# Attention steps 3 to 6 each followed by two half tiles of the first layer, and the row statistics of tile 2 made once

## The chip, the core and the metric

The program runs on one core of a Trainium2 chip. The core has five engines that work side by side and wait for each other through semaphores: TensorE (PE) multiplies matrices and writes to PSUM, VectorE (DVE) and ScalarE (ACT) do elementwise work, GpSimd (POOL) does a little of it, and SyncE (SP) issues most transfers between HBM and SBUF. The metric is the device time of one execution in microseconds (us); lower is better.

## What is computed

Three stages, each on the result of the one before, all in fp32:

```python
# 1 attention with a decaying state: B=4, H=8, S=768, D=64
for t in range(S):
    state = gamma * state + einsum('bhd,bhe->bhde', k[:, :, t], v[:, :, t])
    y[:, :, t] = scale * einsum('bhd,bhde->bhe', q[:, :, t], state)
x = y.transpose(0, 2, 1, 3).reshape(3072, 512)
# 2 first feed-forward block, d_ff = 1024
h = x @ w_in
sm = exp(h - h.max(-1)) / (sum(exp(h - h.max(-1)), -1) + 1e-9)
solu = h * sm
ln = (solu - mean(solu)) / sqrt(var(solu) + 1e-6) * g_ln
x = ln @ w_out
# 3 second feed-forward block, d_ff = 2048
h = x @ w_in2
out = (h * cos(h)) @ w_out2
```

## The kernel before

The attention is cut into 24 **steps** of 64 positions for two batches and all heads (`step`, called by `attend`). A step multiplies its queries with the state, its masked scores with the values, adds its keys and values to the state (`S`) and, in its second half, makes the scores (`sc`) of the next step. On PE it is 64 rows of the order, 128 matmuls of 64x64 in the trace (lines L409, L415, L427). Its result `y` is split by ACT into a high part `xh` and by DVE into a low part `xl`; the two are tile n of the first layer, 128 tokens. Tiles 2 and 3 keep them in `o1h` and `o1l`.

The **first layer** (`mm1`, L633) takes a tile in two halves, c = 0 and c = 1, of 512 columns each: 12 matmuls of 128x512 into one PSUM bank (`xh` times `w1h`, `xl` times `w1h`, `xh` times `w1l`, for four k). Tiles 0, 2 and 4 write to the three banks of `hB`, the others to the two of `hA`. Tile 0 has banks 0 and 1 of `hB`, tile 2 banks 1 and 2, so that the c = 0 half of tile 2 takes the bank of tile 0's c = 1 half. `norm` (L643) makes the row statistics of a whole tile: a maximum on DVE (`sm`, L651), an exponential on ACT (`u`), a product on DVE (`u<-u,hB`, L362), a square on ACT (`junk`), a power on POOL, a normalisation on ACT or DVE (L664), with small one-column operations between. Its product is the last that reads the bank. `first(n, c)` does one half and calls `norm` when c is 1; `chunk` does a quarter of a half and calls `norm` when c is 0 and the last k is done.

The normalised tiles are transposed on PE (`transp`, L678, into `tr`, whose banks take the place of `hB`), split by ACT and DVE into `lt`, and multiplied by the second layer's weights (`mm2`, L703, into `y1`). Beside this ACT and DVE convert weights out of 64-bit words (`convert`, `split_w`): first those of this block (`big`), then those of the second block (`raw`, `wt`, stages `st`), which go back to HBM and are read there from some 320 us on. The second block (L879, L960) fills the rest of the time.

What sets the order: nothing is issued as it is written. Every operation goes into a `Plan`, which holds PE's order to the written one but for a window of 10, and picks on the other engines what can start first and has the longest tail. It works with costs in its own tables; `FETCH` tells it how long PE waits for the next block of 256 instructions, with its first number a time at which the cost changes. The instructions are then built engine by engine in the order found, and each engine runs its own in that order. So a call that is moved in the text moves PE's work directly and reorders the other engines.

Of the kernel before, what the change touches and what calls it, by code (L numbers as in the profile page):

```python
# [32 lines left out]
KD = DM // 128  # L33
# [15 lines left out]
class Plan:  # L49
# [17 lines left out]
    LOOK = .1  # L67
    FIRST = (16, 0.97, 0.6)
    BLOCK = (63, 256)
    FETCH = (30.0, 6.3, 4.0)  # L70

    def __init__(self):
        self.ops = []
# [49 lines left out]
    def order(self):  # L123
# [62 lines left out]
        while left:  # L186
# [36 lines left out]
            if e == "PE":  # L223
# [3 lines left out]
                if fetched[0] // self.BLOCK[1] > was:  # L227
                    blocks.append(max(t + occ, blocks[-1]) + self.FETCH[1 if t < self.FETCH[0] else 2])
            else:
# [28 lines left out]
def body(ctx: ExitStack, tc: tile.TileContext, qkv, consts,  # L258
# [126 lines left out]
    def prep(n):  # L385
        i = steps[n][1]
        if i:
            P.add("POOL", 1.2, lambda: nc.gpsimd.tensor_tensor(  # L388
                out=a_p[n % 2].rearrange("p (a b) t -> p a b t", b=2),
                in0=a_q[n % NA].rearrange("p (a b) t -> p a b t", b=2),  # L390
                in1=gat.unsqueeze(2).to_broadcast([128, NHP, 2, C]), op=ALU.mult),
                [("gat",), ("in", n % NA, 1)], [("x32", n % 2)], port=True)
        if has_state(n):
            k = a_kn[n % NA]
            for a in range(NHP):
                f = cs[:, 1, i, a:a + 1]
                act(k[:, a], k[:, a], AF.Copy, [("cs",), ("in", n % NA, 2)], [("ks", n % NA, a)], 0.295,
                    alt=("DVE", 0.2, lambda k=k[:, a], f=f: nc.vector.tensor_scalar(
                        out=k, in0=k, scalar1=f, scalar2=None, op0=ALU.mult), True), scale=f)
# [225 lines left out]
    def mm1(n, c, k, ms=(0, 1, 2)):  # L625
        h, hk = hbank(n, c)
        xh, xl = xhs[xb(n)], xls[xb(n)]
        xhk, xlk = xk[xb(n)]

        def mm():  # L630
            for m in ms:
                a, lo = ((xh, 0), (xl, 0), (xh, 1))[m]
                nc.tensor.matmul(out=h, lhsT=a[:, k], rhs=w1[lo][k][c], start=(k + m == 0), stop=(k == KD - 1 and m == 2))  # L633
        r = [xhk]
        if 0 in ms or 1 in ms:
            r += [("w1h", k, c)]
        if 1 in ms:
            r += [xlk]
        if 2 in ms:
            r += [("w1l", k, c)]  # L640
        P.add("PE", 0.2267 * len(ms), mm, r, [hk], lat=0.2267 * len(ms) + 0.25, ni=2 * len(ms))
# [374 lines left out]
    def load_to(n):  # L1016
        while loaded[0] <= min(n, ns - 1):
            load_step(loaded[0])
            loaded[0] += 1
# [6 lines left out]
    def weights(n):  # L1026
        for _ in range(min(n, len(wq))):
            f, args = wq.pop(0)
            f(*args)
# [3 lines left out]
    def attend(ahead=True):  # L1033
        n = nxt[0]
        if n >= ns:
            return
        nxt[0] += 1
        if n > 3:
            load_to(n + 1)
        if n + 1 < ns and ahead:  # L1040
            prep(n + 1)
        step(n, ahead)
        if n == ns - 1:
            p2["sb_hook"] = [P.add("HOOK", 0.0, open_sb, lat=0.0, after=P.using({"in", "ag", "asc", "ast", "sc", "S", "y", "wt", "stg", "top"}))]

    def first(n, c):
        for k in range(KD):
            mm1(n, c, k)
        if c == 1:
            norm(n)  # L1050

    def chunk(c, k, tiles=(0, 1)):
        for ms in ((0, 1), (2,)):
            for n in tiles:
                mm1(n, c, k, ms)
                if c == 0 and k == KD - 1 and 2 in ms:
                    norm(n)
# [18 lines left out]
    attend()  # L1076
    for k in range(KD):
        chunk(1, k, (1,))
    attend(False)
    P.chained(True)  # L1080
    load_to(4)
    P.chained(False)
    for k in range(KD):
        chunk(0, k, (0,))
    first(2, 1)
    prep(3)
    scores(3)
    for k in range(KD):
# [3 lines left out]
    attend()  # L1092
    first(2, 0)
    norm(2)
    attend()
    first(3, 0)
    attend()
    first(3, 1)
    weights(len(wq))
    first(4, 0)  # L1100
    first(4, 1)
    attend()
    first(5, 0)
    transp(0, 0)
    transp(0, 1)
    first(5, 1)
    attend()
    transp(0, 2)
    transp(0, 3)
    mm2(0, 0, None, range(2))  # L1110
# [149 lines left out]
```

## Time and profile before

| | |
|---|---|
| median of 3 runs | 839.0 us (837.82 to 840.07) |
| profiled execution | 837.1 us, span 835.3 us |
| PE busy | 817.4 us, 98% of the span |
| DVE, ACT, POOL busy | 649.0, 506.4, 48.6 us |
| transfers | 188.19 MB, mean 225 GB/s |

The span goes from the first to the last instruction; the profiled execution's own time is 1.8 us longer. Attention and first block fill it to about 318 us, the second block from there on. Busy time of PE is modelled and counts matmuls that overlap, so its share is no measure of how tight its work stands: that is read from the starts of its matmuls, and from the time in brackets that a row of the timeline shows when the engine was idle before it.

### The profile page before, as it was taken

The page shows a single profiled execution, that of the slowest core. Times are in us where ns is not written, and L with a number is a line of the kernel's source. Part 1 is how long each engine was busy: PE and PEld are TensorE (multiplying, and loading weights), DVE is VectorE, ACT ScalarE, POOL GpSimd, SP SyncE. Part 2 cuts the span into 40 slices and gives each one's busy share as a digit, 9 for nine tenths or more (in the row PEclk, how much of TensorE's full clock was granted, in tenths as well). Part 3 has the DMA queues.
Part 4 walks back from the last instruction along what each step waited for, and adds up shares of the span by engine and source line. Part 5 has one row for each costly group of instructions (what it writes and reads, how often), then busy time and mean ns, then how long its engine had stood idle before and what let it go on. Part 6 is the DMA issues. An engine that isn't in the chain of part 4 may idle for free.

```text
span 835.3 us, 18919 instructions
## 1 busy us (share of the span) xinstructions
PE 817.4 (98%) x7312; PEld 717.0 (86%) x7312; DVE 649.0 (78%) x1157; ACT 506.4 (61%) x893; POOL 48.6 (6%) x56
## 2 busy tenths in 40 slices
PE   5899999999999999999999999999999999999997
PEld 4778888888888888888889999888999988889997
DVE  4789988879888677338789993787999648779953
ACT  4688857656666466346785463676746446665452
POOL 2221210111101000000000000000000000000000
PEclk9999999999999999999999999999999999999999
DMA  9893699899976649246665688767667787666563
GB/s 353 326 336 114 194 320 342 270 322 300 323 271 224 219 161 319 86 131 195 192 207 184 198 257 246 233 192 197 201 195 209 198 271 194 196 191 188 181 193 83
DMA packets 93513, 188.19 MB, mean 225 GB/s; under 512 B 9712, under 2 KB 25328, under 8 KB 93424
## 3 DMA queue, kind: packets, MB, share of 16 engines
q1 hardware_dynamic: 92816, 186.41, 70.1%
q8 instruction: 58, 0.95, 0.5%
q10 hardware_dynamic: 608, 0.57, 0.2%
q14 instruction: 31, 0.25, 0.1%
HBM read 145.01 MB, written 41.94 MB: 224 GB/s over the span
## 4 chain that ended last, share of the span: by engine, by line
PE 90%; DMA 4%; DVE 3%; SPq 1%; ACT 1%; issue 1%; ACTq 0%
PE U L879 27%; PE pa L960 15%; PE hA L633 13%; PE y L703 11%; PE U L960 8%; PE pb L960 4%; PE y L427 4%; PE hB L633 2%; PE tr L678 2%; PE tr L703 2%; DMA big<-w_in_dram 1%; DMA in<-qkv_dram 1%; PE sc L409 1%; DVE u L362 1%; DMA y1d<-ys 1%
## 5 line engine op out<-in xcount | busy, mean ns | idle before, releaser
L960 PE MATMUL pa<-wr,gh 128*128 128x256 f32 x768 | 139.8, 283 | 0.0
L902 ACT ACTIVATE gh<-A 128x512 fp32r<-128x512 f32 x144 | 90.7, 630 | 78.6 <-PE pa L960 43.6
L904 DVE TENSOR_TENSOR gl<-A,gh 128x512 fp32r<-128x512 f32 x144 | 98.6, 686 | 29.7 <-ACT gh L902 29.6
L960 PEld LDWEIGHTS pa<-wr,gh 128*128 128x128 f32 x768 | 120.2, 192 | 0.5
L960 PE MATMUL pa<-wr,gl 128*128 128x256 f32 x384 | 108.7, 283 | 0.0
L703 PE MATMUL y<-lt,o1h 128*128 128x512 f32 x304 | 101.9, 399 | 0.0
L960 PEld LDWEIGHTS pa<-wr,gl 128*128 128x128 f32 x384 | 73.7, 192 | 0.0
L960 PE MATMUL U<-wr,gh 128*128 128x256 f32 x384 | 70.3, 283 | 0.0
L703 PEld LDWEIGHTS y<-lt,o1h 128*128 128x128 f32 x304 | 57.1, 188 | 12.2
L633 PE MATMUL hA<-w1h,xh 128*128 128x512 f32 x160 | 64.4, 403 | 0.3 <-DVE u L362 0.2
L633 PE MATMUL hA<-w1l,xh 128*128 128x512 f32 x160 | 62.5, 391 | 0.0
L633 PE MATMUL hA<-w1h,xl 128*128 128x512 f32 x160 | 62.4, 390 | 0.0
L960 PEld LDWEIGHTS U<-wr,gh 128*128 128x128 f32 x384 | 59.9, 192 | 0.0
L703 PE MATMUL y<-lt,o1l 128*128 128x512 f32 x152 | 59.3, 390 | 0.0
L351 ACT ACTIVATE st<-wt 128x512 fp32r<-128x512 f32 (+1 forms) x60 | 35.8, 601 | 33.7 <-DMA wd<-st 17.8
L960 PE MATMUL U<-wr,gl 128*128 128x256 f32 x192 | 54.3, 283 | 0.0
L354 DVE TENSOR_TENSOR st<-wt,st 128x512 fp32r<-128x512 f32 (+1 forms) x60 | 40.5, 678 | 17.0 <-ACT st L351 16.8
L427 PE MATMUL y<-s,in 64*64 64x64 f32 x736 | 45.0, 226 | 1.1 <-DVE s L354 1.1
L427 PEld LDWEIGHTS y<-s,in 64*64 64x64 f32 x736 | 36.4, 138 | 9.2 <-issue 4.6
L427 PE MATMUL y<-x,st 64*64 64x64 f32 x672 | 40.3, 218 | 0.0
L388 POOL TENSOR_TENSOR x<-in,c_all 128x512 f32<-128x512 f32 x22 | 30.5, 1385 | 141.2 <-issue 88.2
L960 PEld LDWEIGHTS U<-wr,gl 128*128 128x128 f32 x192 | 36.9, 192 | 0.0
(180 smaller groups left out, 2082.6 us busy)
## 6 DMA issues: line engine op xcount, KB each, us to landing
wr<-wd SPq DMA_DIRECT2D x168, 256.0 KB, 3.0
wr<-td SPq DMA_DIRECT2D x168, 256.0 KB, 3.0
in<-qkv_dram SPq DMA_DIRECT2D x48, 512.0 KB, 6.2
wd<-st SPq DMA_DIRECT2D x28, 512.0 KB, 4.9
td<-st SPq DMA_DIRECT2D x24, 512.0 KB, 3.5
raw<-w_in_dram SPq DMA_DIRECT2D x16, 511.8 KB, 6.0
raw<-w_out_dram SPq DMA_DIRECT2D x16, 511.8 KB, 5.0
y1d<-ys SPq DMA_DIRECT2D x24, 256.0 KB, 3.7
```

What stands on the lines that cost most here:

```text
L351: return P.add("ACT", occ, lambda: nc.scalar.activation(out=out, in_=in_, func=func, **kw), r, w, lat, alt=alt)
L354: return P.add("DVE", occ, lambda: nc.vector.tensor_tensor(out=out, in0=a, in1=b, op=op), r, w, port=port)
L362: return P.add("DVE", occ, lambda: nc.vector.scalar_tensor_tensor(out=out, in0=a, scalar=s, in1=b, op0=op0, op1=op1, **kw), r, w, port=port)
L388: P.add("POOL", 1.2, lambda: nc.gpsimd.tensor_tensor(out=a_p[n % 2].rearrange("p (a b) t -> p a b t", b=2), in0=a_q[n % NA].rearrange("p ( ...
L427: nc.tensor.matmul(out=ybank(n)[0][o, j], lhsT=a[r, j], rhs=b[r, j], start=not part, stop=bool(part) or not later)
L633: nc.tensor.matmul(out=h, lhsT=a[:, k], rhs=w1[lo][k][c], start=(k + m == 0), stop=(k == KD - 1 and m == 2))
L678: nc.tensor.transpose(out=trs[s][:, t * 128:(t + 1) * 128], in_=us[(4 * g + t) % UBUF].rearrange("p c f -> p (c f)")[:, j * 128:(j + 1) * ...
L703: nc.tensor.matmul(out=y1(), lhsT=w[:, j, ds], rhs=lts[j][:, a], start=(j + m == 0), stop=(j == K1 - 1 and m == 2))
L879: nc.tensor.matmul(out=U(), lhsT=p2["wr"][w][:, kk, lo], rhs=p2["x"][m][xl][:, kk], start=(kk + q == 0 and m in (0, 1, 4)), stop=(kk == 1 ...
L902: P.add("ACT", 0.54, lambda: nc.scalar.activation(out=p2["gh"][i], in_=src(), func=AF.Copy), [key], [("gh", i)], after=(*p2["cos_hook"], * ...
L904: P.add("DVE", 0.6, lambda: nc.vector.tensor_tensor(out=p2["gl"][i], in0=src(), in1=p2["gh"][i].bitcast(F32), op=ALU.subtract), [key, ("gh ...
L960: nc.tensor.matmul(out=o, lhsT=p2[x][g][:, t * 128:t * 128 + 128], rhs=v[:, lo], start=(fresh and t % 2 == 0 and i == 0), stop=(s == 7 and ...
```

## The change

In the text of the program's order, four things:

- `attend(False)`, step 2, moves from behind tile 1's c = 1 half to behind the first half of tile 0's c = 0 half.
- `first(2, 1)`, the c = 1 half of tile 2 with a `norm` behind it, becomes four calls of `chunk` with c = 1, which call no `norm`. The other `norm(2)`, behind the c = 0 half, stays.
- Steps 4 to 6 come later: an `attend()` behind tile 2 goes, the next ones stand behind the c = 0 half of tiles 3, 4 and 5, and the one behind tile 5 goes. So 7 steps in place of 8 are done ahead of the loop, and from tile 6 on each step stands one tile closer to its own tile.
- The planner's `FETCH` goes from (30.0, 6.3, 4.0) to (60.0, 5.8, 4.5).

```diff
-    FETCH = (30.0, 6.3, 4.0)
+    FETCH = (60.0, 5.8, 4.5)
...
     for k in range(KD):
         chunk(1, k, (1,))
-    attend(False)
     P.chained(True)
     load_to(4)
     P.chained(False)
-    for k in range(KD):
+    for k in range(2):
         chunk(0, k, (0,))
-    first(2, 1)
+    attend(False)
+    for k in range(2, KD):
+        chunk(0, k, (0,))
+    for k in range(KD):
+        chunk(1, k, (2,))
     prep(3)
...
     first(2, 0)
     norm(2)
-    attend()
     first(3, 0)
     attend()
     first(3, 1)
     weights(len(wq))
     first(4, 0)
+    attend()
     first(4, 1)
+    first(5, 0)
     attend()
-    first(5, 0)
     transp(0, 0)
     transp(0, 1)
     first(5, 1)
-    attend()
```

PE near 22 us, at the end of step 1 (its result goes to `hA_135`). Before, step 2 (`in2`, into `y_173`) follows at once:

```order
L427 MATMUL hA_135<-x32_1_112,st1_169 64x64 x2
L409 MATMUL sc_171<-in2_164 64x64 x2
L427 MATMUL y_173<-s0_166,in2_164 64x64 x2
L415 MATMUL S_172<-in2_164 64x64 x2
L427 MATMUL y_173<-x32_0_111,st0_168 64x64 x2
```

After, tile 1 (`xh1`, `xl1`) follows:

```order
L427 MATMUL hA_135<-x32_1_112,st1_169 64x64 x2
L409 MATMUL sc_171<-in2_164 64x64 x2
L633 MATMUL hA_135<-w1h01_86,xh1_127 128x512
L633 MATMUL hA_135<-w1h01_86,xl1_129 128x512
L633 MATMUL hA_135<-w1l01_94,xh1_127 128x512
```

Tile 1's 12 matmuls went from the middle of step 2 to its front, right behind the step that makes `xh1` and `xl1`.

DVE at the row statistics of tile 0 (`sm0`, `u0`) and of tile 2 (`sm2`, `u2`). Before:

```order
L651 TENSOR_REDUCE sm0_77<-hB_139 128x1
L651 TENSOR_REDUCE sm2_79<-hB_139 128x1
L354 TENSOR_TENSOR s1_167<-sc_171,c_all_170 128x256
L362 SCALAR_TENSOR_TENSOR u0_104,sm0_77<-u0_104,hB_139 128x1024
L362 SCALAR_TENSOR_TENSOR u2_106,sm2_79<-u2_106,hB_139 128x1024
L651 TENSOR_REDUCE sm1_78<-hA_135 128x1
```

After:

```order
L354 TENSOR_TENSOR o1l_125<-y_173,o1h_124 128x512
L651 TENSOR_REDUCE sm0_77<-hB_139 128x1
L354 TENSOR_TENSOR s1_167<-sc_171,c_all_170 128x256 x2
L398 TENSOR_SCALAR in1_163<-in1_163,c_all_170 128x128 x2
L362 SCALAR_TENSOR_TENSOR u0_104,sm0_77<-u0_104,hB_139 128x1024
```

The maximum and the product of the incomplete tile 2 are gone from between tile 0's and tile 1's.

PE behind the c = 0 half of tile 2 (`hB_139`, `o1h_124`). Before, step 4 (`in0`) follows:

```order
L633 MATMUL hB_139<-w1h30_91,o1h_124 128x512
L633 MATMUL hB_139<-w1h30_91,o1l_125 128x512
L633 MATMUL hB_139<-w1l30_99,o1h_124 128x512
L427 MATMUL y_173<-s0_166,in0_162 64x64 x2
L415 MATMUL S_172<-in0_162 64x64 x2
```

After, the c = 0 half of tile 3 (`hA_135`), and step 4 behind its 12 matmuls:

```order
L633 MATMUL hB_139<-w1h30_91,o1h_124 128x512
L633 MATMUL hB_139<-w1h30_91,o1l_125 128x512
L633 MATMUL hB_139<-w1l30_99,o1h_124 128x512
L633 MATMUL hA_135<-w1h00_85,o1h_124 128x512
L633 MATMUL hA_135<-w1h00_85,o1l_125 128x512
```

So steps 4, 5 and 6 each stand 12 matmuls later against the tiles, and two half tiles lie between one and the next.

## Rows read from the trace of the kernel before

**Rows 1.** The page: span, busy time by engine, granted clock in 40 slices.

```profile
span 835.3 us, 18919 instructions
PE 817.4 (98%) x7312; PEld 717.0 (86%) x7312; DVE 649.0 (78%) x1157; ACT 506.4 (61%) x893; POOL 48.6 (6%) x56
PEclk9999999999999999999999999999999999999999
```

**Rows 2.** PE's timeline: start us, length us, instruction, [idle before <- releaser].

```profile
22.52 0.27 PE L427 MATMUL y<-s,in 64*64 64x64 f32 x2 [0.57 <-DVE s L354]
...
41.56 0.50 PE L633 MATMUL hB<-w1h,o1h 128*128 128x512 f32 x1 [1.66 <-DVE u L362]
...
132.65 0.33 PE L678 MATMUL tr<-ident,u 128*128 128x128 f32 x1 [0.30 <-DVE lt L690]
...
308.98 0.50 PE L633 MATMUL hA<-w1h,xh 128*128 128x512 f32 x1 [0.22 <-DVE u L362]
```

**Rows 3.** The chain of waits, 34 to 42 us: start us, length us, what.

```profile
34.36 2.36 DVE sm L651 x2
...
36.81 2.31 ACT u L351 x4
...
39.14 2.38 DVE u L362 x4
```

**Rows 4.** Instructions on `u`, 30 to 50 us: count, duration ns min/median/max, starts.

```profile
L351 ACT ACTIVATE junk<-u,sm x3: 1138/1150/1150, 45.7 to 49.1; 128x1024 bf16<-128x1024 f32 x3
L351 ACT ACTIVATE u<-hB,sm x2: 1105/1111/1117, 36.8 to 37.9; 128x1024 f32<-128x1024 f32 x2
...
L664 DVE TENSOR_SCALAR u<-u,sm x1: 814/814/814, 49.8 to 49.8; 128x1024 f32<-128x1024 f32 x1
```

**Rows 5.** Timelines of ACT, DVE and PE behind step 1.

```profile
21.98 0.60 ACT L351 ACTIVATE xh<-hA 128x512 fp32r<-128x512 f32 x1 [2.26 <-PE sc L409]
...
22.91 0.68 DVE L354 TENSOR_TENSOR xl<-hA,xh 128x512 fp32r<-128x512 f32 x1
...
23.64 0.50 PE L633 MATMUL hA<-w1h,xh 128*128 128x512 f32 x1
```

**Rows 6.** PE's timeline at the gap without a releaser.

```profile
53.23 0.40 PE L633 MATMUL hA<-w1h,o1l 128*128 128x512 f32 x1
53.46 0.39 PE L633 MATMUL hA<-w1l,o1h 128*128 128x512 f32 x1
55.64 0.39 PE L633 MATMUL hA<-w1h,o1h 128*128 128x512 f32 x1 [1.79 <-issue]
```

**Rows 7.** Instruction queue q8 (packets, MB, share): span; windows 46:47, 53:54, 59:61.

```profile
q8 instruction: 58, 0.95, 0.5%
...
q8 instruction: 1, 0.02, 6.0%
...
q8 instruction: 1, 0.02, 5.8%
...
q8 instruction: 1, 0.02, 2.9%
```

**Rows 8.** Timelines of DVE and PE at the first transposes.

```profile
66.33 1.21 DVE L362 SCALAR_TENSOR_TENSOR u<-u,hB 128x1024 f32<-128x1024 f32 x1
...
67.69 1.06 PE L678 MATMUL tr<-ident,u 128*128 128x128 f32 x8
```

**Rows 9.** Busy us by window, with granted clock, DMA share and GB/s last.

```profile
30.00:62.00 32.00, 28.55 (x510) 22.95 (x510) 24.95 (x59) 22.82 (x49) 7.38 (x7) 1.00 0.85 305
62.00:80.00 18.00, 17.78 (x324) 14.64 (x322) 18.00 (x29) 15.39 (x30) 3.69 (x4) 1.00 0.43 145
```

**Rows 10.** Timelines of DVE and PE behind step 13.

```profile
153.00 0.69 DVE L354 TENSOR_TENSOR xl<-y,xh 128x512 fp32r<-128x512 f32 x1
...
153.93 0.39 PE L633 MATMUL hA<-w1h,xl 128*128 128x512 f32 x1
```

**Rows 11.** DVE's timeline: a wait for a load of `in`.

```profile
129.89 0.48 DVE L398 TENSOR_SCALAR in<-in,c_all 128x128 f32<-128x128 f32 x2 [2.36 <-DMA in<-qkv_dram]
```

More of the change, by code (lines that the diff above doesn't have):

```diff
@@ L1082, in body @@
     P.chained(False)
+    for k in range(2):
+        chunk(0, k, (0,))
+    attend(False)
+    for k in range(2, KD):
+        chunk(0, k, (0,))
     for k in range(KD):
-        chunk(0, k, (0,))
-    first(2, 1)
+        chunk(1, k, (2,))
     prep(3)
```

## The prediction, made before the change was run

> **What bounds the kernel now.** I read the profile's page first [rows 1]. The program ran 835.3 us, TensorE (PE) was busy for 817.4 of them and its granted clock reads nine tenths or more in every slice, so it ran at the upper of its two levels, 2.4 GHz. Matmuls overlap in the trace, so busy time alone could hide waits; I therefore took PE's timeline and compared the starts of neighbouring matmuls. A 128x512 matmul starts 0.23 us after the one before it (53.23 and 53.46 in [rows 6]), a whole attention step takes 2.1 us, and from 27 us to the last matmuls there are only four places where PE starts late: 1.66 us at 41.56, 1.79 us at 55.64, 0.30 us at 132.65 and 0.22 us at 308.98 [rows 2]. The change keeps every matmul, so it can only win back waits: these four are 3.97 us, and all that it brings must come from them, less what new waits it makes. Ahead of 22 us nothing on PE moves; after 310 us the work is the same and follows the first part.
>
> The wait at 41.56 is explained by the chain of waits [rows 3]. From 34.36 on, with the first issued half of tile 2 through, VectorE (DVE) makes two row maxima (2.36), ScalarE (ACT) two exponentials (2.31) and DVE two products (2.38), one after the other, and only then may PE overwrite `hB` with the second half of tile 2. One of each pair belongs to tile 0; the other is `norm(2)` called out of `first(2, 1)`, on a tile of which half is missing.
>
> The wait at 55.64 has no releaser ("issue"), so nothing that the program waits for ended there. What the trace shows is instruction traffic: queue q8 moved 58 packets of together 0.95 MB, 16 KB each [rows 7]. PE has 7312 matmuls and as many weight loads [rows 1]; 14,624 instructions over 58 packets are 252 each, and with PE's own wait instructions about 256. An attention step is 128 matmuls in the trace, that is 256 instructions or one packet, and it is used up in 2.1 us. One such packet passed in the window 46 to 47 us and one in 53 to 54, and PE went on 1.6 to 2.6 us after the second began. Counting back from the gap, 6 matmuls (12 instructions) and all but the first 12 instructions of step 5 make one packet, so that block was entered at about 50.3 and the next one could be run at 55.64: **fetching took 5.3 us there**.
>
> The Trainium skill ("Runtime: NRT & Kernel Launch", section Instruction fetch mechanics) says that the sequencer fetches the next 16 KiB page while it runs the current one and that crossing costs "one DMA tail-bump, mostly hidden". The block size agrees with the 16 KB here, "mostly hidden" doesn't at 55.64. By that rule the new order would meet no such gap; that is a rival below.
>
> **The change part by part.** I go along PE, with starts of before as the clock.
>
> 1. *Tile 1's half ahead of step 2.* Before, PE put half of step 2 at 22.52, after 0.57 us of wait, and tile 1's 12 matmuls at 23.64 [rows 2, 5]. Now the 12 come first, and their second matmul reads `xl`, which DVE writes from 22.91 on (0.60 until the next one starts at 23.51); `xh` is there at 22.58. PE is free at 21.95, can do one matmul at about 22.6 and the next at 23.6: 0.65 + 0.70 of wait in place of 0.57, so **about 0.75 lost**. It can't be a gain, since `xl` follows the same rows on DVE; at most 1.0 lost.
>
> 2. *The duplicate goes, tile 0 ends earlier.* Removed on DVE: a maximum and a product of 1.2 each (half of what the chain shows for two), the normalisation 0.8, and some eight one-column operations of some 0.07, together 3.7 us at most; on ACT an exponential and a square, 1.1 each [rows 3, 4]. More important: tile 0's last half is now issued 1.5 to 2 us ahead of the first half of tile 2, so its maximum can start near 31.7, its product ends near 35.2, and `hB` is free 5 us before PE wants it (near 40.4). **1.66 gained**, and no next wait takes its place at that point: the exponent and product of tile 1, needed for tile 3's half in `hA` that now follows at once, end by my count near 42.5, PE comes at 43.3. This margin of 0.8 us is what covers it; without it up to 0.8 comes back.
>
> 3. *Instruction blocks at steps 4 and 5.* Twelve matmuls (24 instructions) now stand ahead of step 4, and half a tile ahead of step 5. Counted on from the boundary before, one block begins 18 instructions into step 4 and ends 9 matmuls behind it: 1.95 + 2.1 = 4.1 us of PE work. The next holds 15 matmuls and most of step 5: 3.4 + 1.85 = 5.2. A fetch of 5.3 makes 1.2 + 0.1 = **1.3 of waits in place of 1.79**, a gain of 0.5. The bounds: the block entered near 45.0 found its packet in the window 46 to 47, so it was there by 49.6 at the latest (4.6) and could be after 2.6; the one entered at 55.64 has its packet in the window 59 to 61, so up to 8 us. At 2.6 both waits vanish, at 8 they are 6.7, at 6.5 (the middle of that window) 3.7. I take 5.3, the only one measured at a gap and between the ends.
>
> 4. *First transposes.* They need the normalised tiles 0 to 3 and the last product on `hB` (tile 4). Before, they stood at 67.69, 0.27 behind the pitch, because that product ran 66.33 to 67.47 [rows 8]. From 62 to 80 us DVE was busy 18.00 of 18.00 us [rows 9], so PE can't run far ahead of it. The duplicate's time on DVE fell into a time when DVE was partly idle; by counting DVE's new order, tile 4's product ends near 65.1, when PE has done 12 instead of 15 matmuls of tile 5. PE would be there at 64.7: 0.4 in place of 0.27, **0.1 lost**. If PE comes later, through part 3, this wait shrinks, so the two cover each other.
>
> 5. *Each step one tile later.* Before, step n+1 stood between step n and the first layer of tile n; now tile n follows step n directly, with 12 or 24 second-layer matmuls (2.7 or 5.4 us) and partly 8 transposes (0.87) between. So `xh`, `xl` of a step are needed at once. The trace shows the chain behind such a step, step 13 [rows 10]: DVE writes `xl` from 153.00 on, some 0.60 net, and the second matmul of the next tile starts at 153.93. The margin is 0.3 us, and in the new order a 0.60 us weight split stands in that row at step 12. Steps 12, 16 and 20 have only the 12 matmuls: I take 0.1 each, **0.3 lost**.
>
> 6. *Later waits.* The 0.30 at 132.65 came from DVE waiting 2.36 us on a load of `in` [rows 11]; the order there is another now, and the 0.22 at 308.98 is covered by the last step, which moves from 290 us to that place. **0.5 gained.** Against it, step 10 now begins where a block begins and nearly fills it: 2.1 to 3.0 us of work against a fetch of 2.6 to 5.3. A full step inside one block cost before only when the boundaries fell on both sides; I take **0.4 lost** (0 to 3.2).
>
> Sum: 1.66 + 0.5 + 0.5 gained, 0.75 + 0.1 + 0.3 + 0.4 lost: 1.1 us. The profiled execution took 837.1 us for a span of 835.3; the median of the three runs is 839.0 (837.82 to 840.07), so the profile is 1.9 below the median. 837.1 becomes 836.0, and on the median's level 839.0 becomes **837.9 us**.
>
> The weight conversion, the queue of loads on SP and the second phase I cost at nothing: the conversion's loads now start some 6 us earlier, for they no longer stand behind an `in` load that waits for step 5, and nothing on PE reads the converted weights ahead of 336 us.
>
> **Rivals.** *A, the fetches hide.* For it: all blocks between 56 and 310 us show no gap; against it: the 1.79. Then 1.3 and 0.4 stay away, the wait at the transposes grows by 0.2, and with 2.6 us gained it is 836.4. (This is what the rule on that page of the Trainium skill gives.) *B, the fetches run long*: 6.5 us each, as loads pile up there (the DMA share is 0.85 between 30 and 62 us [rows 9]): 3.7 instead of 1.3, of which part 4 covers 0.4, and it is 839.9; at 8 us each 842.9. *C, slower: just-in-time `xl`.* DVE waited 2.36 us for a load of `in` at 129.89 [rows 11], one of three such waits over 1.5 us between 110 and 170, and PE hardly noticed, since a step's result had a whole tile of time. With 0.3 of margin such a wait ahead of `xl` goes through. Seven tiles have the short cover (11, 12, 15, 16, 19, 20, 23); at 0.8 us each 5.6 are lost, 843.2. It decides from 0.5 us each on. *D, the change does less than it says*: the planner orders by its own costs and a wait of about the old size stands elsewhere before 85 us, so that nothing moves: 839.0.
>
> **How the numbers follow.** Forecast 0.42; A 0.19; B 0.17; C 0.08; D 0.14. About 0.3% (2.5 us) is what a measurement of this kernel can tell from no change. The forecast, D and most of B lie within it; A lies on the edge, and about all of A with a tail of the forecast makes faster 0.19; slower is C and the long end of B, 0.10; within 0.3% the rest, 0.71. The range goes from 835.9 (A without the 0.3 and 0.2 of parts 5 and 4) to 840.8 (a little beyond B); it leaves out C, B's long end and a thin end below.
>
> **What would show it.** Right: the chain of waits has one maximum and one exponential ahead of tile 2's second half and no gap there; the matmul `hA<-w1h,xh` near 22.6 with its neighbour a microsecond later; a gap without releaser of 0.5 to 2 us between 46 and 57; first transposes between 65 and 66.5; gaps of a few tenths in front of tiles 12, 16 and 20 ended by `xl`; the whole rest of PE's timeline shifted by about a microsecond. Wrong: gaps without releaser that sum to over 3 us or to nothing before 60 us, a gap at tile 3's first half (part 2's margin), or gaps of half a microsecond and more ended by `xl` or by a load of `in` after 85 us.

## The result, and the profile after

The changed kernel takes 846.29 us in the median (845.95 to 850.07), the kernel before beside it 838.62 us: a ratio of 1.010, with an interval of 1.007 to 1.013. It is slower by 7.7 us, where the prediction had 837.9 us and a range up to 840.8. The profiled execution took 846.28 us for a span of 844.5, 9.2 more than before. The page of the changed kernel begins (span, busy time by engine, granted clock):

```profile
span 844.5 us, 18911 instructions
...
PE 820.5 (97%) x7312; PEld 717.8 (85%) x7312; DVE 649.8 (77%) x1160; ACT 497.9 (59%) x877; POOL 51.9 (6%) x55
...
PEclk9999999999999999999999999999999999999999
```

Against [rows 1] hardly anything shows: the same 7312 matmuls, and every slice reads 9. One has to go to PE's waits. The list of what PE waited for in the changed kernel (total us, times, longest us):

```profile
PE sc L409 <- DMA in<-qkv_dram: 5.7, 1, 5.7
PE y L427 <- issue: 3.1, 1, 3.1
PE tr L678 <- DVE lt L690: 1.8, 2, 1.0
PE hA L633 <- DVE xl L354: 1.7, 1, 1.7
PE hB L633 <- ACT w1h L351: 1.7, 1, 1.7
PE hB L633 <- DVE u L362: 1.4, 1, 1.4
PE hB L633 <- ACT u L351: 1.3, 1, 1.3
PE tr L678 <- ACT ys L708: 1.2, 1, 1.2
...
PE hB L633 <- DVE sm L651: 0.3, 1, 0.3
```

Without its first row (the first load) the list sums to 13.4 us; the same list of before sums to 7.5. So 5.9 of the 9.2 us are waits that the view names. In PE's timeline (start, length, instruction, idle before it and what ended it) the first five stand here, in place of the first rows of [rows 2]:

```profile
22.50 0.50 PE L633 MATMUL hA<-w1h,xh 128*128 128x512 f32 x1 [1.70 <-DVE xl L354]
...
32.24 0.47 PE L633 MATMUL hB<-w1h,o1h 128*128 128x512 f32 x1 [0.33 <-DVE sm L651]
34.93 0.50 PE L633 MATMUL hB<-w1l,o1h 128*128 128x512 f32 x1 [1.29 <-ACT u L351]
37.99 0.50 PE L633 MATMUL hB<-w1l,o1h 128*128 128x512 f32 x1 [1.40 <-DVE u L362]
...
61.53 0.27 PE L427 MATMUL y<-s,in 64*64 64x64 f32 x2 [3.06 <-issue]
```

The wait at 41.56 is gone, as foreseen, but three waits of together 3.0 us stand between 32 and 38, inside the 12 matmuls of tile 2's c = 1 half. ACT and DVE show the other side of them: the maximum, the exponential and the product of tile 0.

```profile
30.87 1.23 DVE L651 TENSOR_REDUCE sm<-hB 128x1 f32<-128x1024 f32 x1 [0.26 <-PE hB L633]
...
33.67 1.11 ACT L351 ACTIVATE u<-hB,sm 128x1024 f32<-128x1024 f32 x1 [2.63 <-PE hB L633]
...
36.70 1.22 DVE L362 SCALAR_TENSOR_TENSOR u<-u,hB 128x1024 f32<-128x1024 f32 x1 [3.56 <-PE hB L633]
```

The maximum is done at 32.1, yet the exponential, which needs nothing else of tile 0, starts at 33.67 and waited for PE, and PE then waited for it. They take turns: PE, ACT, PE, DVE, PE. But tile 0 reads banks 0 and 1 of `hB`, and the matmuls write bank 2.

The gap at 61.53 is the successor of the one in [rows 6], with a cost behind it that the slices of the page hide. Windows on PE in the changed kernel (busy us and count of PE, PEld, DVE, ACT, POOL, then granted clock, DMA share, GB/s):

```profile
58.47:61.53 3.06, 0.00 (x0) 0.00 (x0) 1.43 (x3) 2.33 (x5) 0.00 (x0) 1.00 0.85 340
61.53:63.20 1.67, 1.67 (x21) 1.38 (x21) 1.13 (x2) 1.19 (x2) 1.09 (x1) 0.99 0.28 91
63.20:66.60 3.40, 3.40 (x10) 2.67 (x9) 3.03 (x7) 1.97 (x4) 1.13 (x2) 0.51 0.83 294
66.60:70.00 3.40, 3.40 (x63) 2.64 (x64) 3.40 (x5) 3.16 (x8) 0.00 (x0) 1.00 0.01 2
```

From 63.2 to 66.6 the granted clock was at its lower level, 1.2 GHz: from 63.19 to 66.59 the matmuls start 0.41 to 0.43 apart in place of 0.23, eight times in a row. That is 8 times 0.2, or 1.6 us more. The Trainium skill ("TensorE: Matmul & The Clock Gate", section Part 1: The HAM clock gate) says that the half rate is the default and that activity lifts it; the two levels here, 0.51 and 1.00, agree.

So of 9.2 us, 5.9 are named waits and 1.6 the lower clock; 1.7 lie in many small delays that the list doesn't name.

### The profile page after: what moved, and what is told of

It is laid out like the page before. It is cut to its first block, busy times and chain, and to the rows that moved or that the text cites. A ratio compares the mean times of both kernels' runs of the same rounds, so it can differ in the third digit from the quotient of the medians.

```text
span 844.5 us, 18911 instructions
## 1 busy us (share of the span) xinstructions
PE 820.5 (97%) x7312; PEld 717.8 (85%) x7312; DVE 649.8 (77%) x1160; ACT 497.9 (59%) x877; POOL 51.9 (6%) x55
## 4 chain that ended last, share of the span: by engine, by line
PE 67%; DMA 2%; DVE 1%; ACT 0%; SPq 0%; issue 0%; ACTq 0%
PE U L879 27%; PE pa L960 16%; PE U L960 8%; PE y L703 4%; PE pb L960 4%; PE hA L633 4%; PE tr L703 2%; DMA raw<-y1d 2%; PE tr L678 1%; PE y L427 1%; DMA out_dram<-oo 0%; DVE u L664 0%; DVE lt L690 0%; DVE raw L354 0%; SPq L823 0%; DVE oo L935 0%
## 5 line engine op out<-in xcount | busy, mean ns | idle before, releaser
L690 DVE TENSOR_TENSOR lt<-tr,lt 128x512 fp32r<-128x512 f32 x48 | 31.2, 684 | 9.6 <-ACT lt L688 9.4
```

Source lines behind the costliest of these rows:

```text
L690: P.add("DVE", 0.6, lambda: nc.vector.tensor_tensor(out=lts[j][:, 1], in0=trs[s], in1=lts[j][:, 0].bitcast(F32), op=ALU.subtract), [("hb", ...
```

## Experiments

All ratios are to the kernel before, run beside it, with their intervals; where a kernel ran once (tile cut, two more loads, the second look, store ahead) there is no interval, and its time stands beside 840.55 us, one run of the kernel before. "Changed kernel" is the kernel of this case. So that places can be compared, the table gives by how much PE falls behind the kernel before in each stretch of the profiled execution: the work that it has left at a time (its matmuls still to come, at their usual distances), less what the kernel before had left at that time. The three columns add up to the difference of the spans and are good to about half a microsecond; a minus means that PE is ahead. The profiled execution of the kernel before took 837.1 us, 1.5 less than its median beside the changed kernel, so all sums stand that much high. What stands ahead of 26 us also differs between executions of one program (-0.5 and 0.8 in the changed kernel).

| | ahead of 26 us | 26 to 68 us | behind 68 us | span |
|---|---|---|---|---|
| step 2 alone (b_step2) | 1.7 | 7.0 | 1.4 | 10.1 |
| duplicate out alone (b_dup) | 0.0 | 1.3 | 1.0 | 2.3 |
| steps 4 to 6 alone (b_steps) | -0.3 | -0.1 | 2.0 | 1.6 |
| FETCH alone (b_fetch) | -0.4 | 2.0 | 0.7 | 2.3 |
| duplicate and steps 4 to 6 (b_dupsteps) | 1.2 | 0.4 | 4.6 | 6.2 |
| the same and FETCH (a_back2) | -0.6 | 1.5 | 9.4 | 10.3 |
| changed kernel | -0.5 | 4.6 | 5.0 | 9.2 |
| again (after_2) | 0.8 | 2.3 | 7.0 | 10.1 |
| with the old FETCH (a_fetch) | 0.9 | 1.4 | 6.3 | 8.5 |
| statistics late (e_norm) | 1.2 | 1.3 | 12.6 | 15.1 |
| tile cut (e_split) | 2.0 | -1.1 | 5.9 | 6.8 |
| duplicate out, statistics late (b_order) | 0.0 | 2.9 | 4.0 | 6.9 |
| loads held (e_hold) | 0.6 | 0.3 | 6.4 | 7.3 |
| two more loads (b_more) | -0.2 | 0.6 | 0.9 | 1.2 |
| store ahead (a_ring) | -0.3 | 1.4 | 4.4 | 5.5 |
| statistics late, loads held (e_both) | 0.3 | -1.1 | 11.6 | 10.8 |
| the same, old FETCH (e_both_f) | 0.7 | -2.7 | 5.7 | 3.7 |
| the same, store ahead (a_all) | 0.7 | -3.0 | 4.8 | 2.4 |
| the same, step 2 back (b_all) | -0.3 | -2.2 | 6.8 | 4.3 |

### The parts one by one

Step 2's move alone:

```diff
-    attend(False)
...
-    for k in range(KD):
+    for k in range(2):
+        chunk(0, k, (0,))
+    attend(False)
+    for k in range(2, KD):
         chunk(0, k, (0,))
```

> The kernel before, with only step 2 moved behind the first half of tile 0's c = 0 half. Theory 1: this move alone brings the waits on hB, since the window of PE's order no longer lets tile 2's matmuls pass tile 0's last: about 3 us of waits between 31 and 39, and about 1.1 more ahead of tile 1's half at 22.5; the wait near 41.5 for the duplicate statistics stays in part. About 841.5 us (840 to 843.5). Rival 1: the move costs no more than the wait for tile 1's xl (0.75 to 1.1), and the waits on hB come from the duplicate's absence: 839.5.

847.67 us, 1.0103 (1.0076 to 1.0130): as slow as the whole change, and slower than either answer. Two rows of its timeline:

```profile
37.21 0.50 PE L633 MATMUL hB<-w1h,o1h 128*128 128x512 f32 x1 [1.30 <-ACT u L351]
...
59.99 0.47 PE L633 MATMUL hA<-w1l,o1h 128*128 128x512 f32 x1 [3.00 <-issue]
```

Waits on `hB` between 31 and 39 are there as theory 1 has it, but of 0.33 and 1.30, about half of its 3. Beside them stand the wait of 1.70 for `xl`, a gap without a releaser of 3.00 with a stretch at the lower clock behind it, and three more waits on `hB` (1.16 at 44.77 for the statistics of tile 2, 1.35 and 1.39 at tile 4). PE's named waits sum to 15.1, without the first load.

The duplicate alone:

```diff
-    first(2, 1)
+    for k in range(KD):
+        chunk(1, k, (2,))
```

> The kernel before, with only the duplicate statistics of tile 2 taken out. Prediction's part 2: the wait of 1.66 at 41.56 is gone and nothing takes its place: 837.0 us. Theory 1: 11 of tile 2's 12 matmuls still come ahead of the maximum of tile 0 and one behind it, so that this one waits some 1.2 us for the maximum; 1.66 gone, 1.2 new: 838.2 us. In both the gap without a releaser near 55 may change with the time at which its block is entered, by up to 1.5 either way.

839.29 us, 1.0002 (0.9987 to 1.0016): nothing. The 1.66 is gone, and one wait stands in its place, as theory 1 had it and against part 2 of the prediction:

```profile
35.40 0.50 PE L633 MATMUL hB<-w1l,o1h 128*128 128x512 f32 x1 [1.32 <-DVE sm L651]
```

Steps 4 to 6 alone (the calls moved as in the change):

> The kernel before, with only steps 4 to 6 moved behind the half tiles. The wait of about 1.7 at 41.5 stays (duplicate in, step 2 in its old place). Gap without a releaser between 50 and 62: by theory 2 it follows from how many loads are issued ahead of the fetch, between 0 and 3. Theory 3: behind 68 us 3 to 6 us are lost, 842 to 845 us; rival 3: next to nothing is lost there, 838.5 to 840.

839.00 us, 1.0004 (0.9995 to 1.0013): nothing, rival 3. FETCH alone:

> The kernel before, with only the planner's FETCH at its new numbers. PE's work and its order up to 60 us stay but for a few rows. Theory 4 (the new numbers alone make the planner put ACT's, DVE's and SP's work behind 68 us in an order that serves PE worse): 3 to 7 us are lost behind 68 us, among them waits of about 1 us each at transposes near 335 to 345 for ys and lt, as in all four kernels with the new numbers so far: 842 to 846 us. Rival 4 (the numbers do nothing; the loss comes of the duplicate's absence and steps 4 to 6 together, since each alone lost nothing): 838 to 840.

840.85 us, 1.0014 (0.9999 to 1.0029): nothing that can be told from no change; theory 4 falls in this form.

Then pairs. The changed kernel with step 2 at its old place:

> The changed kernel with step 2 put back to its old place; the duplicate is out, steps 4 to 6 are late. Theory 1 (step 2's move brings the waits on hB, since steps in front of tile 0's last matmuls take up the window in which tile 2's matmuls could pass them): of the three waits on hB only one of about 1.3 is left, as where the duplicate alone was taken out, and no wait of 1.7 ahead of tile 1's half. Up to 68 us PE then lies as in that kernel. Theory 3 (steps 4 to 6 behind their tiles make the later work just in time): behind 68 us 3 to 6 us are lost: 842 to 845 us. Rival 3 (the later loss is only what any shift of the planner's order does): 839 to 840.

845.83 us, 1.0084 (1.0056 to 1.0111). Of the waits on `hB` for statistics one of 1.32 is left, as expected, but 9.4 us are lost behind 68 us. The same with FETCH's old numbers:

> The kernel before without the duplicate and with steps 4 to 6 late, FETCH at its old numbers: the kernel of 845.8 us (step 2 put back) less the new numbers. Theory 4: the waits behind 68 us (9.8 us there) fall to 1 to 2: 838 to 840. Rival 4: the two parts together lose what neither loses alone, 845 again.

842.60 us, 1.0031 (1.0016 to 1.0046): half of it. The changed kernel with FETCH's old numbers:

> The changed kernel with FETCH at its old numbers. The waits on hB (3.0) and the one ahead of tile 1's half stay, and the gap near 60 too, since the loads come in the same order. Theory 4: behind 68 us only 1 to 2 us are lost in place of 6.6, and the waits near 340 are gone: 840 to 842 us. Rival 4: 846 again.

846.95 us, 1.0088 (1.0065 to 1.0110): no gain. So one part, step 2's move, costs the whole by itself, and yet 7 us of the loss stay when it alone is taken back: the parts don't add up. The others cost nothing each; the duplicate and steps 4 to 6 together cost 2 to 3 us; and FETCH matters in some company (4.4 us by the ratios, 1.0084 against 1.0031) and not in other.

### The waits on hB

The statistics of tile 0 written behind tile 2's matmuls:

```diff
...
     for k in range(2, KD):
-        chunk(0, k, (0,))
+        chunk(0, k, (0,), False)
     for k in range(KD):
         chunk(1, k, (2,))
+    norm(0, [len(P.ops) - 1])
```

> The changed kernel, with one thing moved: the row statistics of tile 0 are put into the program behind the 12 matmuls of tile 2's c = 1 half, not between them. Theory 1: PE and the statistics of tile 0 let each other wait, since both use the one PSUM tile hB and the program's order goes from one to the other and back, though they touch different banks. Then the three waits at 32.24, 34.93 and 37.99 (0.33, 1.29, 1.40; 3.0 together) are gone, the 12 matmuls run in one piece of 2.7 us, the maximum of tile 0 starts right behind them, near 35, and the product ends near 38.7, before PE wants hB again near 39.5. The gap without a releaser stays of about its size, since the loads issued ahead of it come 3 us earlier too: 843.3 us (842.5 to 844). Rival 1: the statistics of tile 0 are simply too slow for the new order, and the wait moves to tile 2's c = 0 half near 40: 846.

851.86 us, 1.0156 (1.0128 to 1.0184). The mechanism came as theory 1 has it and the time didn't. Two rows of DVE:

```profile
36.81 1.22 DVE L651 TENSOR_REDUCE sm<-hB 128x1 f32<-128x1024 f32 x1 [1.79 <-PE hB L633]
...
39.31 1.22 DVE L362 SCALAR_TENSOR_TENSOR u<-u,hB 128x1024 f32<-128x1024 f32 x1 [1.08 <-ACT u L351]
```

The 12 matmuls run from 33.76 to 36.39 without a gap, the maximum follows at 36.81, and nothing waits for the product. Between 26 and 68 us the kernel wins 3.3 us, as expected; behind 68 us it loses 7.6 more, among it 2.62 us at 146.88, where PE waited for ACT, which itself had stood 2.77 us without a releaser.

The test that cuts the tile:

```diff
-    hB = psb.tile([128, 3, 512], F32, name="hB")
+    hB = psb.tile([128, 2, 512], F32, name="hB")
+    hC = psb.tile([128, 512], F32, name="hC")
...
-            return hB[:, b], ("hB", b)
+            return (hC if b == 2 else hB[:, b]), ("hB", b)
```

> The changed kernel with hB cut into a PSUM tile of two banks and one of a single bank, hC; tile 2's c = 1 half goes to hC, and the maximum, exponential and product of tile 2 are made in two halves each. Order as in the changed kernel: the statistics of tile 0 still stand in the program between tile 2's matmuls. Theory 1: PE and these statistics no longer share a PSUM tile, so that neither waits for the other: the 12 matmuls run in one piece from about 32 on, ACT's exponential follows DVE's maximum at once (about 32.1 in place of 33.7), the product ends near 34.7 in place of 37.9. Rival 1 (they wait for banks, ports or speed, not for the tile): the gaps at 32 to 38 stay. Time about 843, if the gap of the fetch stays 3.

Its timelines (DVE, ACT, and PE's first and last of the 12 matmuls; the maximum stands 2.8 us later here than in the changed kernel, from a later start):

```profile
33.72 1.23 DVE L664 TENSOR_REDUCE sm<-hB 128x1 f32<-128x1024 f32 x1 [0.26 <-PE hB L634]
...
34.98 1.13 ACT L352 ACTIVATE u<-hB,sm 128x1024 f32<-128x1024 f32 x1 [1.08 <-DVE sm L664]
...
36.22 1.22 DVE L363 SCALAR_TENSOR_TENSOR u<-u,hB 128x1024 f32<-128x1024 f32 x1 [0.22 <-ACT u L352]
...
34.69 0.50 PE L634 MATMUL hC<-w1h,o1h 128*128 128x512 f32 x1
...
37.31 0.39 PE L634 MATMUL hC<-w1l,o1h 128*128 128x512 f32 x1
```

Maximum, exponential and product follow each other at once while PE writes `hC` without a gap. The banks are the same as in the changed kernel, and so is PE's order there; tile 2's statistics, made in halves, come later. What the expectation has wrong is the program's order. The plan makes one order of the instructions of all engines together, not one for each engine, and the semaphores follow that one. In the changed kernel it has the maximum of tile 0, five of tile 2's matmuls, the exponential, six matmuls, the product, one matmul: one wait of PE at each of the three places. With the tile cut it has the maximum, all 12 matmuls, the exponential, the product. Even so the exponential starts at 34.98, when the first of the 12 had just begun, and waits for none of them; with one tile, in the run before this one, the maximum that stood behind the 12 waited for the last (36.81). So the waits come from two tiles of tokens sharing one PSUM tile: **the semaphores are set by the tile, in the order of the program, not by the bank**. 843.92 us, beside 840.55 for the kernel before.

On the kernel without the duplicate, the same reordering of the statistics:

> The kernel before without the duplicate, and with the statistics of tile 0 put behind all of tile 2's 12 matmuls. Theory 1: the one wait of 1.32 for the maximum that stood in place of the 1.66 at 41.56 is gone too, and nothing else: 838.0 us (837 to 839), 1.3 below the kernel without the duplicate. Rival: the product of tile 0 then ends later and the wait comes back at tile 2's c = 0 half near 40: 839.3.

842.18 us, 1.0032 (1.0016 to 1.0048). The 1.32 is gone, but the gap without a releaser at 56.99 is 3.09 us, with the lower clock behind it, where the kernel without the duplicate had three of 0.81, 0.69 and 0.58 (46.19, 51.99, 56.81). What was won at one place was lost again, and more, at others: behind 68 us it waits 1.91 for `u` at 101.79, 0.66 at 118.64 and 1.00 at 341.20.

### The gap without a releaser

That these gaps are fetches shows in where they stand. In the 20 profiles of this case 23 gaps without a releaser (of 0.15 us and more, behind 22 us) are on PE, and every one is in front of its 606th, 734th or 862nd matmul (in one kernel the 861st), 128 matmuls or 256 instructions apart, whatever the order of the work; and in every one PE goes on 2.2 to 2.5 us after a packet of the instruction queue began to pass.

Before, that packet passed between 53.0 and 53.5, 3.0 us after PE entered the block ahead of it (50.27). In the changed kernel PE, counted in the same way, entered the block at 53.08 and went on at 61.53; the instruction queue's packet (packets, MB, share) is in the half microsecond from 59.0:

```profile
q8 instruction: 1, 0.02, 11.7%
```

Five loads of 0.5 MB, two of `in` and three of `raw`, had been issued from 50.92 to 53.2. The three later ones held back:

```diff
+    gate, loads_of = [], {}
+
     def load_step(n):
+        loads_of[n] = len(P.ops)
...
-                (128, 2 * (hi - lo)), w=rk if n >= SMALL else rk[x:x + 1], bulk=n >= K1)
+                (128, 2 * (hi - lo)), w=rk if n >= SMALL else rk[x:x + 1], bulk=n >= K1, after=tuple(gate) if n < 2 * K1 + 3 else ())
...
+        if n == 8:
+            gate.append(loads_of[9] + 1)
+            weights(len(wq))
...
-    weights(len(wq))
+    weights(2)
     first(4, 0)
```

> The changed kernel, with one thing moved: the first three loads of the second block's weights (raw, 0.5 MB each, issued at 51.8 to 53.2) are put on SP's queue behind two more loads of in, so that they are issued after 62 us. PE's work is the same. Theory 2: the gap of 3.06 at 61.53 is a fetch of instructions that had to stand behind the 2.5 MB of loads issued from 50.9 to 53.2; its packet passed between 59.0 and 59.5, 6 us after PE had entered the block before. With 1.0 MB instead, the packet passes 2 to 3.5 us after that block is entered, the gap is gone, and with it the stretch from 63.2 to 66.6 at a granted clock of 0.51, which cost 1.6: 841.6 us (840.5 to 843), unless conversions that start 10 us later cost something behind. Rival 2: the gap is set by how little PE work lies in the block (5.2 us) against a fetch that takes 8 whatever else is in transit: the gap stays near 3, 846.

844.99 us, 1.0073 (1.0047 to 1.0099). SP, PE and a window of it:

```profile
61.19 2.60 SPq L509 DMA_DIRECT2D raw<-w_in_dram  x3
...
59.92 0.27 PE L430 MATMUL y<-s,in 64*64 64x64 f32 x2 [0.20 <-issue]
...
61.60:65.00 3.40, 3.40 (x17) 2.81 (x16) 3.05 (x7) 1.99 (x4) 1.13 (x2) 1.00 0.93 333
```

With the loads issued at 61.19 the gap is 0.20 in place of 3.06 and the clock stays at 1.00. This is no scatter: at the same matmul, the 862nd, the eight profiles without the duplicate, with late steps and with these loads in their place have 1.41 to 3.06 us, the five with the loads held 0.20 and less. The loads in transit set the gap. How, the opposite test was to tell: two more loads, which nobody reads, ahead of the same fetch in the kernel before.

```diff
+        if n == 14:
+            at = [len(P.ops) - 1]
+            dma(lambda: [nc.sync.dma_start(out=raws[x].bitcast(I16)[:, 0:2047], in_=src[:, 1:2048]) for x in range(2)],
+                (128, 8188), w=[("raw", x, h) for x in range(2) for h in (0, 1)], after=at)
```

> The kernel before with two more loads of 0.5 MB each, of data that nobody reads, behind the loads that are issued from 48.0 to 48.9. Theory 2 (the fetch stands behind the loads in transit): at the 390 GB/s of that stretch 1.0 MB is 2.7 us, so the packet of the fetch that passed between 53.0 and 53.5 passes near 56, and the gap at 55.64 grows from 1.79 to about 4.4 us; after a gap of that size the granted clock halves for some 3.4 us. Rival 2: the gap stays near 1.8.

```profile
48.78 1.50 SPq L510 DMA_DIRECT2D raw<-w_out_dram  x2
...
56.26 0.39 PE L637 MATMUL hA<-w1h,o1h 128*128 128x512 f32 x1 [2.49 <-issue]
```

The gap grew by 0.70, not by 2.6; the packet passed between 54.0 and 54.5, 0.8 us later. So the fetch doesn't stand behind all bytes that were asked for before it, and theory 2's arithmetic falls. Its direction isn't shown by this run: the next one shows that the gap of one and the same program differs by 0.9 from one execution to another. The time, 838.38 us, shows no loss.

The changed kernel again:

> The changed kernel unchanged, a second look. The three waits on hB and the one for xl should come again to a tenth of a microsecond, since only engines wait for each other there; the gap without a releaser near 61 within half a microsecond of 3.06, if the loads in front of it set it; of the waits near 250, 340 and 344 I expect those at 340 and 344 again, and the one at 250 to differ by some tenths, since it starts from a load of in.

847.26 us. The waits on `hB` and the one for `xl` came again to the hundredth (1.70, 0.33, 1.29, 1.40). The gap was 2.15, without a drop of the clock; in two other kernels with the same work and loads there (a_ring and a_fetch) it was 1.46 and 1.41. So 3.06 and the 1.6 behind it belong to one execution; the three others have 1.4 to 2.2. The waits near 340 and 345 came again (1.09 and 1.39), those between 68 and 320 wandered: 0.51 at 70.67, 0.40 at 111.88, 0.84 at 226.18 and 0.68 at 259.60 in place of 0.98 at 249.81.

### Behind 320 us

In the changed kernel SP, ACT and PE show near 340:

```profile
326.74 5.91 SPq L823 DMA_DIRECT2D wr<-wd  x8
333.03 0.32 SPq L709 DMA_DIRECT2D y1d<-ys  x1
...
339.54 0.60 ACT L708 ACTIVATE ys<-tr 128x512 f32<-128x512 f32 x1 [3.97 <-DMA y1d<-ys]
...
340.19 0.66 PE L678 MATMUL tr<-ident,u 128*128 128x128 f32 x4 [1.19 <-ACT ys L708]
```

There is one buffer `ys`. Its store stood on SP behind eight loads for the second block, and landed 6.4 us later. With the later half of these loads behind the store:

```diff
-        dma(lambda: nc.sync.dma_start(out=y1d[g][:, d], in_=ys), (128, 2048), [("ys",)], [("y1d", g, d)], occ=0.4)
+        p2["kept"] = dma(lambda: nc.sync.dma_start(out=y1d[g][:, d], in_=ys), (128, 2048), [("ys",)], [("y1d", g, d)], occ=0.4)
...
-                after=p2["ring_hook"])
+                after=(*p2["ring_hook"], *([p2["first"]] if 6 < loads[0] <= NWR else ())))
...
+    p2["first"] = p2["kept"]
     load_x(0)
     load_ring(NWR)
```

> The changed kernel, where the loads 7 to 14 of the second block's first weights (wr) are put behind the store of ys that was issued at 333.03. Theory 5: that store was late twice, on SP behind eight wr loads (issued 326.7 to 332.6) and then behind their 2 MB in transit (landing after 6.4 us), and ACT's next copy to ys waited 3.97 us for it. Now it is issued near 331.7 and lands within 4.5 us, and the waits at 340.19 (1.19) and 344.15 (0.79) go: 2 us less, 844. Rival 5: they come from DVE's and ACT's order and stay.

842.62 us, beside 847.26 for the unchanged one, one run each. ACT no longer waits:

```profile
334.56 0.60 ACT L708 ACTIVATE ys<-tr 128x512 f32<-128x512 f32 x1
```

Both waits on PE are gone: 2.0 us by the rows of the changed kernel's profile, 2.5 by those of after_2. Theory 5 holds. Of the rest of the 4.6 us, 0.7 is the smaller gap of that run (1.46 for 2.15) and 1.3 its start (the wait for `xl` ends at 22.55 in place of 23.88).

### All of it

Both front repairs, first with FETCH's new numbers, then with the old:

> The changed kernel with both repairs: the statistics of tile 0 behind tile 2's half, and the first three raw loads behind two more loads of in. Theories 1 and 2 together: no waits on hB between 32 and 39, no gap over 0.5 near 58 and no stretch at half the granted clock: up to 68 us PE is 7 to 8 us ahead of the changed kernel. If the later part is as with the held loads alone, 838.5 to 840.5. Rival: what is won ahead of 68 us is given back behind, as where only the statistics were moved (8 us lost there): 844 to 847.

850.02 us, 1.0140 (1.0122 to 1.0158). Ahead of 62 us as expected: no waits on `hB` for statistics, no gap. Behind, four waits for `u` (7.1 together, one of 2.61 with the lower clock behind it), and the ones near 340: the rival.

> The changed kernel with the statistics of tile 0 behind tile 2's half, the first raw loads behind two more loads of in, and FETCH at its old numbers. Ahead of 68 us it should lie as with both repairs and the new numbers, 4 to 5 us ahead of the changed kernel and about level with the kernel before. Theory 4: behind 68 us 1 to 2 us lost: 838 to 839.5. Rival 4: 846 to 850 again, as with the new numbers.

842.01 us, 1.0038 (1.0021 to 1.0054): some 8 us better by FETCH alone, though FETCH did nothing that can be told in the kernel before and in the changed one.

With the repair near 340 too:

> The changed kernel with all that was found taken away: the statistics of tile 0 behind tile 2's half, the first raw loads behind two more loads of in, the wr loads 7 to 14 behind the store of ys, FETCH at its old numbers. The same without the last edit took 842.0; the edit on wr took about 2.4 us out of the stretch from 332 to 344: 839.5 us (838.5 to 841). What is left against the kernel before is the wait of 1.7 for xl and some losses between 68 and 320.

**838.67 us, 0.9993 (0.9978 to 1.0007): level with the kernel before.** PE's waits in it:

```profile
PE sc L412 <- DMA in<-qkv_dram: 5.7, 1, 5.7
PE tr L681 <- DVE lt L693: 2.8, 2, 1.8
PE hA L636 <- DVE xl L354: 1.7, 1, 1.7
PE hB L636 <- ACT w1h L351: 1.7, 1, 1.7
```

They sum to 8.1 without the first, against 7.5 before: no gap without a releaser, no wait on `hB` for statistics, and in exchange 1.8 at 130.83 for `lt`. With step 2 at its old place:

> The same with step 2 back at its old place. By the prediction's part 1 the move cost the difference of the waits, 1.70 against 0.57, so 1.1 us less than the other one: 838.4 us (837 to 839.5), level with the kernel before or just below. If the move has another price, the two differ by more. Rival: behind 68 us the planner's order differs again and hides the 1.1.

841.50 us, 1.0033 (1.0016 to 1.0050): slower, not faster. The 1.1 that the move costs at 22.5 is saved, but behind 68 us the kernel loses 2.0 more than the other: three waits of 1.11, 0.92 and 0.64 between 188 and 257 (for `lt` and `u`) in place of the 1.8 at 130.83, and smaller delays. This is the rival. No kernel of these beats the one before.

## Why the prediction was wrong, point by point

**What bounds the kernel** was read rightly: the change keeps PE's work, and all goes by waits. What failed is that new ones were looked for only where a resource is known to be shared. Of the 10.3 us between the 836.0 forecast for the profiled execution and its 846.28, part 2 makes 3.0, part 3 3.4 (1.8 of gap and 1.6 of clock), the second phase 2.0, the wait at 249.81 1.0 and part 1 0.4; what is left, small delays less forecast losses that stayed away, nets to 0.5.

**Part 1** (0.75 lost, at most 1.0): 1.13 were, 1.70 in place of 0.57, all of it ahead of the first matmul. That one reads `xh`, not `xl`; but `xl` is made out of `hA`, into whose other bank it writes. By the mechanism found on `hB` it had to wait until DVE had read `hA`. This place was not tested apart; where only `hB` was cut, the wait stayed (1.71).

**Part 2** is the step that failed. "`hB` is free 5 us before PE wants it ... and no next wait takes its place" took banks for the unit of waiting. The statistics of tile 0 and tile 2's matmuls touch different banks of one PSUM tile, and wait for each other in the order of the program: 3.0 us. The planner's keys are banks, so it mixed the two freely. In the kernel before it had let nine of tile 2's matmuls pass tile 0's last one, which reads the `w1l` that DVE made last, so that the statistics came behind them all; with step 2 in front none of tile 2's matmuls gets ahead of tile 0's last, and the maximum goes right behind that one. That the window of 10 makes the difference is argued from these orders; no run widens it. The sign was there before the change: tile 0's maximum started at 34.36, though tile 0's last matmul started at 33.26; it waited for tile 2's, which started at 33.94 (`xh` is tile 0's, `o1h` tile 2's):

```profile
33.26 0.39 PE L633 MATMUL hB<-w1l,xh 128*128 128x512 f32 x1
...
33.94 0.39 PE L633 MATMUL hB<-w1l,o1h 128*128 128x512 f32 x1
...
34.36 2.35 DVE L651 TENSOR_REDUCE sm<-hB 128x1 f32<-128x1024 f32 x2 [2.11 <-PE hB L633]
```

The +1.66 became -1.4.

**Part 3** had the right blocks and mechanism, and rival B the right direction: loads pile up and the fetch runs long. What was wrong is one price, 5.3 us, for both fetches. At the first boundary (53.08), where it had 1.2 of wait, there is none: PE entered the block ahead at 49.05, before the five loads were issued, and the packet began to pass at 50.07. At the second, where it had 0.1, there are 3.06 in the profiled execution and 1.4 to 2.2 in others: there PE entered the block ahead at 53.08, with all five in transit, and the packet began at 59.13. Missing was also the lower clock after the longest gaps. The rule of the Trainium skill ("Runtime: NRT & Kernel Launch", section Instruction fetch mechanics) that crossing is mostly hidden holds where the loads were held back (0.20) and not here.

**Parts 4 and 5**: the first transposes show no wait in the profiled execution, as part 3's size covers it, and 0.51 and 0.87 where the gap was shorter (the second look and a_ring), where part 4 had 0.4. No wait ended by `xl` is in the list behind 22.5, so neither the 0.3 nor rival C came in that form.

**Part 6**: the two waits are gone, and no block costs anything at step 10. But "the second phase I cost at nothing" was wrong by 2.0 to 2.5 us: I asked what reads the converted weights, and not what stands behind their loads on SP.

**Rival D**, the planner, was priced at "nothing moves". Behind 68 us kernels that differ by one edit lose from 0.7 to 12.6 us, by other places of ACT's and DVE's waits. This is the part that stays open: the duplicate's absence and late steps lose nothing each and 2 to 3 us together, and FETCH is worth 4 us beside these two, 8 us with both front repairs, and nothing in the kernel before or the changed one. That it comes through the planner's order is argued from the edits, which touch nothing else; which wait in it decides wasn't found. So taking away the waits that were found doesn't give their sum back: without those on `hB` the changed kernel was some 5 us slower, and the one that is level with the kernel before (838.67) needed the old FETCH too.

## What to carry to other kernels

Before moving statistics or loads against matmuls, ask which instructions share a tile, not which share a bank, and look at the order in which the program names them; two halves that need not wait for each other belong in tiles of their own. A planner that keeps finer keys than the semaphores will hide such waits from itself. When loads move, look at what else stands in their queues: here an instruction fetch and a store of a single buffer.

## What the runs showed of the hardware

- **The clock after gaps.** Between 22 us and the last matmul, the granted clock fell to its lower level at PE gaps of 3.06, 3.09 and 3.00 us, each time; it fell at none of 1.99 and less. In between, it fell at 2.36, 2.61 and 2.62, and not at 2.15 and 2.49. Windows behind the gaps of 3.09 (the duplicate out, statistics late), 2.36 (the changed kernel, statistics late) and 2.49 (two more loads), one row each:

```profile
57.00:60.30 3.30, 3.30 (x8) 2.62 (x9) 1.62 (x2) 0.36 (x1) 0.00 (x0) 0.50 1.02 412
```

```profile
59.80:63.00 3.20, 3.12 (x21) 2.52 (x21) 2.34 (x5) 1.95 (x3) 2.13 (x2) 0.51 0.58 182
```

```profile
57.20:59.00 1.80, 1.80 (x9) 1.49 (x8) 1.80 (x5) 0.58 (x1) 0.00 (x0) 1.00 1.02 419
```

- **The fetch of a block** took 5.4 us from the entry of the block ahead to PE's next instruction in the kernel before, 8.5 in the changed one and 5.6 with the loads held. From the packet to PE going on it is 2.2 to 2.5 in all 23 gaps; what varies is when the packet gets through, 3.0, 6.1 and 3.2 us after the entry in these three.
- **The same program** showed gaps of 3.06 and 2.15 us at the same place, while the four waits between engines ahead of 40 us came again to the hundredth:

```profile
62.01 0.27 PE L427 MATMUL y<-s,in 64*64 64x64 f32 x2 [2.15 <-issue]
```
